# Moving small VectorE and ScalarE work of a four-layer attention kernel to GpSimd, with one load queue and a guarded second program

## The chip, the cores and the metric

The kernel runs on one core of a Trainium2 chip. The metric is device time in microseconds of one launch; the median of a few runs counts. Beside it there is one profiled execution, from which all views of the profile come. Its engines are called PE (TensorE), DVE (VectorE), ACT (ScalarE), POOL (GpSimd) and SP (the engine that issues most DMAs).

## The reference

The input is one sequence of 2048 rows with 512 columns in bfloat16. Four residual layers follow one another: A, B, A, B, where both A layers use the same weights and both B layers use the same weights. There are 32 heads of 16 columns.

```python
def _layernorm(x, axis=-1, eps=1e-5):
    m = jnp.mean(x, axis=axis, keepdims=True); v = jnp.var(x, axis=axis, keepdims=True)
    return (x - m) / jnp.sqrt(v + eps)

def _A_ref(x, wqkv, wo):                       # linear attention
    q, k, v = split(x @ wqkv)                  # (heads, rows, 16)
    phi = lambda t: jnp.where(t > 0, t + 1, jnp.exp(t)) + 1e-6
    pq, pk = phi(q), phi(k)
    kv = einsum("hsd,hse->hde", pk, v);  z = einsum("hsd->hd", pk)
    num = einsum("hqd,hde->hqe", pq, kv)
    den = einsum("hqd,hd->hq", pq, z)[..., None] + 1e-6
    return merge(num / den) @ wo

def _B_ref(x, wqkv, wo):                       # causal window of 256 rows
    q, k, v = split(x @ wqkv)
    scores = einsum("hqd,hkd->hqk", q, k) * (Dh ** -0.5)
    idx = jnp.arange(S)
    mask = (idx[:, None] - idx[None, :] >= 0) & (idx[:, None] - idx[None, :] < 256)
    p = softmax(where(mask, scores, -1e9));  return merge(p @ v) @ wo

x = x + _A_ref(_layernorm(x), A_wqkv, A_wo)
x = x + _B_ref(_layernorm(x), B_wqkv, B_wo)
x = x + _A_ref(_layernorm(x), A_wqkv, A_wo)
x = x + _B_ref(_layernorm(x), B_wqkv, B_wo)
```

## The kernel before

The rows are cut into 16 tiles of 128 rows, which stay in SBUF as `xres` from the first load to the last store. Nothing is a loop on the chip: Python builds a graph of operations, a list scheduler puts every operation on an engine and in an order, and `emit` writes the five instruction streams with semaphore waits. Each engine runs its stream strictly in that order.

The scheduler (`_Sched.schedule`) repeatedly takes, of all operations that could run, the one with the smallest sum of its planned start and `LAM` times its `pick`. `pick` is the operation's place in the graph (about its tile number, counted on through the stages) plus an offset from the table `PLAN`, which has one number for each kind of operation. An operation's engines and assumed times stand beside it, such as `{"DVE": 0.32}`; where two engines are given, the one with the earlier planned start gets it. `LAT` holds the assumed time from the end of an operation on one engine to a start on another. Rings of buffers (`xn`, `E`, `pq`, `kbd`, ...) limit how far one stage may run ahead of the next.

The graph has these stages, which overlap in time:

- "1.": for each tile, layer norm (`ln`), transposition (`transp`), the k and v projections of layer A (`a_kv`), the feature map (`phi`) and the sum of pk and v over all rows (`kv_mm`).
- "2.": for each tile, the q projection of layer A and its output (`a_q`, `a_out`), then layer B's projections (`b_qkv`) and windowed attention (`b_attn`), each ending in `wo`, which transposes, multiplies by the output weight and adds into `xres`. After it "2k." does for the third layer what "1." does for the first.
- "3.": as "2." for the last two layers, with a store of each finished tile.

The lines that matter here:

- `ln`: L587 and L588 take mean and variance on DVE. L589 and L590 form the reciprocal root on ACT as a logarithm and an exponential of one column. L592 normalises into `xn` on DVE. L600 is a DMA transposition issued by SP; L607 is the same on PE for the few tiles listed in `BYPE`.
- `phi`: L647 exponential on ACT into `E`; L648 minimum with one and addition of 1e-6 on DVE, in place; L649 the positive part added on DVE.
- `b_qkv`: L735, two instructions on DVE, multiplies the transposed keys `kT` by two head masks into `kbd`, which is what the scores read. L745 moves `vt` into `vbd` with four DMAs issued by POOL, which wait for the copy at L617.
- `b_attn`: scores on PE (L770, L807), exponentials on ACT (L790, L814), triangular masks as products on DVE (L797 for `pH`, L826 for `pF`), products with v on PE (L838, L850), the reciprocal of the denominators (L860) and the division (L862). The softmax subtracts no maximum.
- `loads`: the 16 row tiles on SP's queue, the weights `w_Ak`, `w_Av`, `w_Aq` on ACT's queue, the other five weights on SP's queue after the rows.
- `consts` and the `fill_` functions: constants and presets, mostly memsets on POOL in the first microseconds.

Of the kernel before, what the change touches and what calls it, by code (L numbers as in the profile page):

```python
# [6 lines left out]
dt = mybir.dt  # L7
# [4 lines left out]
P = 128  # L12
D = 512
# [125 lines left out]
class _Sched:  # L139
# [6 lines left out]
    LAM = 0.033256  # L146
    PAIRS = 4

    def __init__(self, nc, ctx, plan):
        self.nc = nc  # L150
        self.ctx = ctx
        self.plan = plan
        self.ops = []
        self.pools = []
        self.at = ("", 0.0)
        self.handle = {"PE": nc.tensor, "ACT": nc.scalar, "DVE": nc.vector, "POOL": nc.gpsimd, "SP": nc.sync}
# [131 lines left out]
    def emit(self):  # L288
# [39 lines left out]
        sem = {e: self.ctx.enter_context(self.nc.semaphore("s_" + e)) for e in self.ENGS}  # L328
        count = {e: 0 for e in self.ENGS}
        slots = {}  # L330
        for o in order:
            if o.is_dma and getattr(o, "signals", False):
                b = o.refs[-1]
                key = (b.pool.name, b.slot) if b.pool is not None else ("out" if o.final else id(b))
                if key not in slots:
                    slots[key] = [self.ctx.enter_context(self.nc.semaphore("s_dma%d" % len(slots))), 0]
                slots[key][1] += 16 * o.dmas
                o.sem, o.val = slots[key]
# [17 lines left out]
def _dve_cost(n, rate=1):  # L356
# [5 lines left out]
    "1.ln.st": -2.3432, "1.ln.ag": -7.629, "1.ln.ln": 3.7656, "1.ln.rs": -4.4647, "1.ln.xn": -5.7325, "1.ln.xT": -1.1827, "1.ln.xTc": -8.1345, "1.k0":  # L362
    -1.1601, "1.k1": -4.702, "1.k.e": -4.1683, "1.k.m": -6.7525, "1.k.p": -1.6235, "1.v0": 1.4018, "1.v1": 0.4024, "1.vc": -3.4569, "1.kv": -4.203,
    "1.fin0": 2.1358, "1.fin1": -13.6914, "2.q0": 8.2163, "2.q1": 4.674, "2.q.e": 0.348, "2.q.m": 0.4534, "2.q.p": 0.4456, "2.n0": 2.0377, "2.n1":
    -23.4096, "2.da": -0.7298, "2.dr": 2.4131, "2.dm": -1.9393, "2.o.oT": 21.7702, "2.o.w0": 5.1533, "2.o.w1": -9.7692, "2.o.x": 3.8104, "2.b.ln.st":
    4.7152, "2.b.ln.ag": 4.432, "2.b.ln.ln": 1.6702, "2.b.ln.rs": 5.701, "2.b.ln.xn": -1.1144, "2.b.ln.xT": 9.8065, "2.b.k0": 4.5754, "2.b.k1":
    3.6236, "2.b.kc": 2.0847, "2.b.kb": 10.4518, "2.b.q0": 0.8948, "2.b.q1": 2.5577, "2.b.qc": 4.9459, "2.b.v0": 4.9246, "2.b.v1": -12.1234, "2.b.vc":
    5.5499, "2.b.vd": 12.193, "2.a.sH": 0.8556, "2.a.eH0": -2.6845, "2.a.eH1": 0.8974, "2.a.mH0": 0.4401, "2.a.mH1": 3.8097, "2.a.s0": 1.2702,
    "2.a.e00": 1.5581, "2.a.e01": 9.0526, "2.a.m0": -0.62, "2.a.s1": 1.3991, "2.a.e10": 12.4542, "2.a.e11": 7.3125, "2.a.m1": -0.1479, "2.a.s2":
    1.0274, "2.a.e20": 4.7291, "2.a.e21": 4.4722, "2.a.m2": 0.4653, "2.a.s3": 1.7165, "2.a.e30": 1.5475, "2.a.e31": 0.6114, "2.a.m3": -1.3736,  # L370
    "2.a.u0h": 2.7481, "2.a.u00": -34.0427, "2.a.u01": 5.3112, "2.a.dr0": -4.153, "2.a.dm0": -2.6925, "2.a.u1h": 4.975, "2.a.u10": 6.2037, "2.a.u11":
    -18.3104, "2.a.dr1": 6.915, "2.a.dm1": -0.6536, "2.a.o.oT": 14.4848, "2.a.o.w0": 2.4276, "2.a.o.w1": 1.1529, "2.a.o.x": 3.6287, "2.a.o.oTc":
    8.1341, "2k.ln.st": -6.3433, "2k.ln.ag": 0.0878, "2k.ln.ln": 5.2229, "2k.ln.rs": 4.8961, "2k.ln.xn": 3.3782, "2k.ln.xT": 19.3092, "2k.k0": 6.4763,
    "2k.k1": -20.2592, "2k.k.e": -2.6403, "2k.k.m": -3.0627, "2k.k.p": -2.0237, "2k.v0": 6.8601, "2k.v1": 1.882, "2k.vc": 6.6851, "2k.kv": 9.0019,
    "2k.acc": 2.3357, "2k.ln.xTc": -4.0281, "2.fin0": 1.9926, "2.fin1": -9.0356, "3.q0": 17.6187, "3.q1": 11.9424, "3.q.e": -1.6125, "3.q.m": 17.8339,
    "3.q.p": 3.0371, "3.n0": 21.2198, "3.n1": -7.948, "3.da": 12.6926, "3.dr": 3.3151, "3.dm": 6.3971, "3.o.oT": 2.5807, "3.o.oTc": 24.0655, "3.o.w0":
    19.7899, "3.o.w1": 5.4264, "3.o.x": 16.6218, "3.b.ln.st": -10.8173, "3.b.ln.ag": 14.1252, "3.b.ln.ln": 6.9441, "3.b.ln.rs": 21.0639, "3.b.ln.xn":
    12.1622, "3.b.ln.xT": 8.289, "3.b.ln.xTc": 17.8884, "3.b.k0": 15.1594, "3.b.k1": 19.123, "3.b.kc": 14.9965, "3.b.kb": 17.7419, "3.b.q0": 21.072,
    "3.b.q1": 12.1272, "3.b.qc": 18.2848, "3.b.v0": 22.3007, "3.b.v1": 20.3746, "3.b.vc": 17.7903, "3.b.vd": 51.1264, "3.a.sH": 15.3262, "3.a.eH0":
    19.97, "3.a.eH1": 21.9656, "3.a.mH0": 27.1553, "3.a.mH1": 21.5402, "3.a.s0": 14.35, "3.a.e00": 31.3932, "3.a.e01": 18.1646, "3.a.m0": 6.6429,  # L380
    "3.a.s1": 16.293, "3.a.e10": 17.5396, "3.a.e11": 16.9782, "3.a.m1": 24.787, "3.a.s2": 16.1138, "3.a.e20": 20.9056, "3.a.e21": 4.4488, "3.a.m2":
    28.9959, "3.a.s3": 17.2049, "3.a.e30": 0.2397, "3.a.e31": 21.5025, "3.a.m3": 26.0854, "3.a.u0h": 16.3563, "3.a.u00": 5.8543, "3.a.u01": 1.5404,
    "3.a.dr0": 23.5963, "3.a.dm0": 20.2443, "3.a.u1h": 25.5916, "3.a.u10": 15.3421, "3.a.u11": -15.2287, "3.a.dr1": 8.2662, "3.a.dm1": 18.4897,
    "3.a.o.oT": 8.6597, "3.a.o.w0": 26.2182, "3.a.o.w1": 10.8826, "3.a.o.x": 15.5577, "3.a.o.out": -7.4131, "3.a.o.oTc": 16.0395,
}
BYPE = {("x1.", t) for t in range(6)} | {("a2.", 15), ("k2.", 15), ("o3.", 0), ("x3.", 0), ("a3.", 15)}
VMOVE = {"POOL": 2.06}
LATE = 1


class _Kernel:
    def __init__(self, nc, A_x, A_wqkv, A_wo, B_x, B_wqkv, B_wo, out):
# [5 lines left out]
        self.ctx = ExitStack()  # L398
# [13 lines left out]
    def run(self):  # L412
        nc, T = self.nc, self.T
        with self.ctx:
            s = self.s = _Sched(nc, self.ctx, PLAN)
            self.consts()
            self.xres = [_Buf(None, h) for h in self.tiles("xres", T, [P, D])]
            self.stats = self.tiles("stats", 1, [P, T, 6], F32)[0]
            self.mv = self.tiles("mv", 1, [P, T, 2], F32)[0]
            self.rstd = self.tiles("rstd", 1, [P, T], F32)[0]  # L420
            ps = self.ctx.enter_context(nc.psum_tensor("ps", [P, 8, 512], F32))
            self.pG = _Banks("ps", ps)
            s.pools.append(self.pG)
            self.r_xn = self.ring("xn", 4, [P, D])
            self.r_xT = self.ring("xT", 5, [P, 4, P])
            self.r_xTa = self.ring("xTa", T, [P, 4, P])
            self.r_E = self.ring("E", 4, [P, D])
            self.r_pk = self.ring("pk", 8, [P, D])
            self.r_pq = self.ring("pq", 18, [P, 4, P])
            self.r_kvz = self.ring("kvz", 4, [P, 2, 136])  # L430
            self.r_qT = self.ring("qT", 4, [P, 4, P])
            self.r_pF = self.ring("pF", 6, [P, 4, 512])
            self.r_kT = self.ring("kT", 3, [P, 4, P])
            self.r_vt = self.preset("vt", 3, [P, 2, 16, 17], self.fill_vt())
            self.r_o = self.ring("o", 4, [P, D])
            self.r_oT = self.ring("oT", 4, [P, 4, P])
            self.r_dn = self.ring("dn", 4, [P, 32], F32)
            self.kvacc = self.tiles("kvacc", 1, [P, 4, 136], F32)[0]
            self.r_vA = self.preset("vA", 8, [P, 32, 17], self.fill_vA())
            self.r_kbd = self.ring("kbd", 6, [P, 4, 2, P])  # L440
            self.r_vbd = self.preset("vbd", 6, [P, 2, 2, 16, 17], self.fill_vbd())
            self.r_pH = self.preset("pH", 3, [P, 16, 192], self.fill_pH())
            self.loads()
            self.graph()
            s.schedule()
            s.emit()
            done = max((o for o in s.ops if o.final), key=lambda o: o.val)
            nc.sync.wait_ge(done.sem, done.val)
# [36 lines left out]
    def consts(self):  # L485
# [13 lines left out]
        def f_tri(e, en):  # L499
            e.memset(tri[:], 1.0)  # L500
# [31 lines left out]

        s.at = ("", -3)
# [18 lines left out]
    def loads(self):  # L552
# [3 lines left out]
        def dma(key, eng, dst, src, bufs, lat):  # L556
            s.at = ("", key)
            s.op("load", {eng: 0.47}, lambda e, en: e.dma_start(dst, src), writes=bufs, dma=True, tail=lat - s.LAT["SP"][0])

        xv = self.x[0].rearrange("(t p) d -> t p d", p=P)  # L560
        for t in range(T):
            dma(-5 + 0.01 * t, "SP", self.xres[t].h[:], xv[t], [self.xres[t]], 2.4 + 0.2 * t)

        def wload(name, key, eng, c0, c1, lat):
            self._nm = "w_" + name
            h = self.sb([P, 4, c1 - c0])
# [8 lines left out]
        for i, n in enumerate("kqv"):  # L575
            c = "qkv".index(n) * D
            wload("B" + n, -0.9 + 0.01 * i, "SP", c, c + D, 9.0)
# [408 lines left out]
```

## Time and profile before

| | |
|---|---|
| median of 3 runs | 482.95 us (482.86 to 487.02) |
| profiled execution, its own time | 483.88 us |
| span of that execution | 482.6 us |
| mean granted PE clock | 0.968 |
| busy PE, DVE, ACT, POOL | 401.5, 393.7, 384.4, 72.3 us |
| HBM read, written | 6.29 MB, 2.10 MB |

Busy time is the time in which an engine had an instruction under way; the span runs from the first to the last instruction. A group of instructions in the profile gives its line, engine, operation, the tiles written and read with their shapes, the count, the busy time and mean length, and then how long the engine was idle just before such instructions and for whom. The chain of work that ended last is followed back from the last instruction, at each step to whatever released it.

### The profile page before, as it was taken

How to read it: one execution, taken by the hardware profiler on the slowest of the kernel's cores; microseconds unless marked ns; L12 is line 12 of the kernel's file. 1: busy time of each engine (PE TensorE's matmuls, PEld its weight loads, DVE VectorE, ACT ScalarE, POOL GpSimd, SP SyncE). 2: the span in 40 equal slices, each digit the busy share in tenths (PEclk: the TensorE clock that was granted, in tenths of full speed). 3: DMA queues.
4: the chain of work that ended last, by engine and by line, in shares of the span. 5: the costliest groups of instructions: out<-in, count | busy, mean ns of one | idle time of the engine just before them, and what ended most of it. 6: DMA issues, size and time to landing. Idle time of an engine off the chain costs nothing.

```text
span 482.6 us, 18490 instructions
## 1 busy us (share of the span) xinstructions
PE 401.5 (83%) x8173; PEld 279.8 (58%) x8236; DVE 393.7 (82%) x962; ACT 384.4 (80%) x577; POOL 72.3 (15%) x145
## 2 busy tenths in 40 slices
PE   2999898899889898998888887879887878878676
PEld 1546666476666665664655665647665555556444
DVE  6996996989887999885877799789988868877634
ACT  3765367988998889999999446988988878889993
POOL 5000033211211010121100002402211111111100
PEclk9999998999999999997999999999999989999967
DMA  8941252342221223312111012343223343332202
GB/s 270 275 66 23 46 93 56 66 69 47 47 48 37 46 60 66 48 36 48 36 24 25 12 23 55 53 70 55 66 58 58 58 58 58 58 56 48 48 25 45
DMA packets 76656, 29.39 MB, mean 61 GB/s; under 512 B 66336, under 2 KB 74528, under 8 KB 76576
## 3 DMA queue, kind: packets, MB, share of 16 engines
q1 hardware_dynamic: 70896, 22.17, 23.3%
q0 software_dynamic: 4096, 4.46, 5.8%
q10 hardware_dynamic: 1584, 1.57, 1.0%
q8 instruction: 65, 1.06, 1.0%
q14 instruction: 15, 0.12, 0.1%
HBM read 6.29 MB, written 2.10 MB: 17 GB/s over the span
## 4 chain that ended last, share of the span: by engine, by line
DVE 30%; PE 29%; ACT 22%; DMA 16%; issue 2%; SPq 0%
ACT pF L814 15%; PE ps L626 13%; DMA oT<-o 9%; PE ps L638 6%; ACT pH L790 4%; DVE stats L587 4%; DVE xres L657 4%; PE ps L850 4%; DMA xT<-xn 3%; DVE o L717 3%; DVE pF L826 3%; DMA xTa<-xn 3%; PE ps L838 2%; PE ps L807 2%; DVE pq L649 2%
## 5 line engine op out<-in xcount | busy, mean ns | idle before, releaser
L814 ACT ACTIVATE pF<-ps 128x1024 bf16<-128x1024 f32 (+2 forms) x256 | 241.6, 971 | 21.0 <-PE ps L807 18.6
L745 POOL DMA_DIRECT2D vbd<-vt x128 | 66.2, 526 | 377.7 <-DVE vt L617 184.1
L790 ACT ACTIVATE pH<-ps 128x1024 bf16<-128x1024 f32 (+1 forms) x64 | 62.2, 972 | 10.7 <-PE ps L770 9.4
L807 PE MATMUL ps<-qT,kbd 32*128 32x128 bf16 x1920 | 51.9, 223 | 21.2 <-ACT pF L814 12.2
L657 DVE TENSOR_TENSOR xres<-ps,xres 128x512 bf16<-128x512 f32 x64 | 43.6, 683 | 22.8 <-PE ps L626 22.7
L647 ACT ACTIVATE E<-ps 128x512 bf16<-128x512 f32 x64 | 38.2, 597 | 29.7 <-PE ps L638 15.8
L807 PEld LDWEIGHTS ps<-qT,kbd 32*128 32x128 bf16 x1920 | 30.3, 95 | 53.4 <-ACT pF L814 31.4
L850 PE MATMUL ps<-vbd,pF 128*128 128x34 bf16 x1920 | 59.4, 179 | 0.0
L826 DVE TENSOR_TENSOR pF<-pF,const 128x512 bf16<-128x512 bf16 (+1 forms) x128 | 50.8, 398 | 7.3 <-ACT pF L814 6.7
L850 PEld LDWEIGHTS ps<-vbd,pF 128*128 128x128 bf16 x1920 | 53.8, 97 | 0.4
L626 PE MATMUL ps<-w_Bo,oT 128*128 128x512 bf16 x120 | 34.5, 408 | 16.1 <-DMA oT<-o 10.8
L797 DVE TENSOR_TENSOR pH<-pH,const 128x1024 bf16<-128x1024 bf16 (+1 forms) x64 | 41.8, 653 | 7.4 <-ACT pH L790 6.4
L587 DVE BATCH_NORM_STATS2 stats<-xres 128x6 f32<-128x512 bf16 x64 | 43.8, 687 | 3.7 <-DMA xres<-in_A_x_dram 2.5
L838 PE MATMUL ps<-vbd,pH 128*128 128x34 bf16 x960 | 34.9, 179 | 4.7 <-DVE pF L826 2.7
L626 PE MATMUL ps<-w_Ak,xTa 128*128 128x512 bf16 x117 | 32.4, 401 | 6.7 <-DMA xTa<-xn 4.4
L638 PE MATMUL ps<-xT,w_Bk 128*128 128x128 bf16 x512 | 35.9, 221 | 2.0 <-DMA xT<-xn 0.8
L638 PE MATMUL ps<-xT,w_Bq 128*128 128x128 bf16 x512 | 35.5, 223 | 1.8 <-DMA xT<-xn 1.3
L838 PEld LDWEIGHTS ps<-vbd,pH 128*128 128x128 bf16 x960 | 29.6, 97 | 11.8 <-DVE pF L826 4.2
L626 PE MATMUL ps<-w_Ao,oT 128*128 128x512 bf16 x111 | 29.1, 379 | 7.1 <-DMA oT<-o 3.6
L638 PE MATMUL ps<-xTa,w_Aq 128*128 128x128 bf16 x512 | 34.1, 219 | 0.1
L638 PEld LDWEIGHTS ps<-xT,w_Bk 128*128 128x128 bf16 x512 | 30.0, 99 | 6.9 <-issue 1.7
L626 PE MATMUL ps<-w_Av,xTa 128*128 128x512 bf16 x123 | 33.2, 388 | 0.5 <-issue 0.2
(70 smaller groups left out, 544.9 us busy)
## 6 DMA issues: line engine op xcount, KB each, us to landing
vbd<-vt POOLq DMA_DIRECT2D x128, 34.0 KB, 2.4
xres<-in_A_x_dram SPq DMA_DIRECT2D x16, 128.0 KB, 6.4
out_dram<-xres SPq DMA_DIRECT2D x16, 128.0 KB, 1.7
oT<-o SPq DMA_TRANSPOSE x61, 2.5
w_Ak<-in_A_wqkv_dram ACTq DMA_DIRECT2D x1, 512.0 KB, 4.8
w_Av<-in_A_wqkv_dram ACTq DMA_DIRECT2D x1, 512.0 KB, 6.6
w_Aq<-in_A_wqkv_dram ACTq DMA_DIRECT2D x1, 512.0 KB, 8.9
w_Ao<-in_A_wo_dram SPq DMA_DIRECT2D x1, 512.0 KB, 7.0
```

The lines of the kernel that those rows point to most:

```text
L587: s.op(n + ".st", {"DVE": 0.595}, lambda e, en: e.bn_stats(a_st, x.h[:]), reads=[x], writes=[st])
L626: i = e.matmul(g.h, xT.h[:, kt, :], w.h[:, kt, :], start=(kt == 0), stop=(kt == 3), skip_group_check=True)
L638: i = e.matmul(g.h[:, f * P:(f + 1) * P], w.h[:, kt, f * P:(f + 1) * P], xT.h[:, kt, :], start=(f == 0 and kt == 0), stop=(kt == 3), skip_ ...
L657: s.op(n + ".x", {"DVE": _dve_cost(512)}, lambda e, en: e.tensor_tensor(x.h[:], g.h, x.h[:], ALU.add), reads=[g], writes=[x])
L745: return [e.dma_start(vbd.h[64 * a:64 * a + 64, j, a], vt.h[64 * j:64 * j + 64, a]) for a in range(2) for j in range(2)]
L790: return e.activation(d, c, ACT.Exp, bias=0.0, scale=DH ** -0.5)
L797: return e.tensor_tensor(vH(g), vH(g), tr, ALU.mult)
L807: i = e.matmul(ss[r // 2].h[:, r % 2, m * P:m * P + P], kbds[fj[m] // 2].h[32 * r:32 * r + 32, f, fj[m] % 2, :], qT.h[32 * r:32 * r + 32, ...
L814: s.op("e%d%d" % (f, g), {"ACT": _act_cost(2 * (4 - m0) * P)}, lambda e, en, S=ss[g], pb=pb, g=g: e.activation(pb.h[:, 2 * g:2 * g + 2, m0 ...
L826: return e.tensor_tensor(v, v, tr, ALU.mult)
L838: i = e.matmul(U.h[:, c:c + 34], pH.h[:, 4 * r + f, 64 * a:64 * a + P], vbds[j // 2].h[:, j % 2, :, 4 * f + r, :], start=first[0], stop=Tr ...
L850: i = e.matmul(U.h[:, c:c + 34], pFs[f].h[:, r, m * P:m * P + P], vbds[fj[m] // 2].h[:, fj[m] % 2, :, 4 * f + r, :], start=False, stop=Tru ...
```

## The change

Six things change. The reciprocal root is formed on POOL by an addition and a power of minus one half. The key masks go to POOL; `xn` and the first step of the feature map may go to POOL or DVE. All loads go out on SP's queue in one written order. The triangular masks become a minimum with 0 or 3e38. The reciprocals of the softmax denominators are kept for all tiles; their extremes are compared with two limits, a count is formed, and every engine reads it at its end: if it is above zero, a second program with bounded scores runs behind the first. For the given inputs only the first program's work and the branch are executed. Last, the scheduler gets a new `LAM`, a new `PLAN` (every offset differs), a margin of 0.5 us on the assumed time of transpositions and of the `vbd` move, and slightly smaller rings, and SBUF is laid out anew.

```diff
-    LAM = 0.033256
+    LAM = 0.036392
...
 VMOVE = {"POOL": 2.06}
+XN = {"POOL": 0.62, "DVE": 0.32}
+EM = {"POOL": 0.62, "DVE": 0.2}
+KB = {"POOL": 1.2}
 LATE = 1
+SLACK = 0.5
...
+            with ExitStack() as self.ctx:
+                s = self.build()
+                done = max((o for o in s.ops if o.final), key=lambda o: o.val)
+                for e in s.handle.values():
+                    e.wait_ge(self.verdict.sem, self.verdict.val)
+                v = nc.values_load(self.flag[0:1, 0:1], min_val=0, max_val=1 << 20)
+                nc.sync.wait_ge(done.sem, done.val)
+            with nc.If(v > 0):
+                nc.all_engine_barrier()
+                self.safe = True
+                with ExitStack() as self.ctx:
+                    s = self.build()
...
-            self.r_pq = self.ring("pq", 18, [P, 4, P])
+        self.r_pq = self.ring("pq", 17, [P, 4, P])
...
-            self.r_dn = self.ring("dn", 4, [P, 32], F32)
+        self.r_dn = self.ring("dn", 3, [P, 32], F32)
...
-            e.memset(tri[:], 1.0)
+            e.memset(tri[:], BIG)
...
+            dma("SP", h[:], src[:, :, c0:c0 + D], [b], 1.2 if name[1] != "k" and name != "Av" else 0.5, 1.55)
...
+        for k in (0, 1, "Ak", 2, 3, "Av", *range(4, T), "Aq", "Ao", "Bk", "Bq", "Bv", "Bo"):
+            wload(k) if isinstance(k, str) else xload(k)
...
-        s.op(n + ".ln", {"ACT": 0.12}, lambda e, en: e.activation(a_rs, self.mv[:, t, 1:2], ACT.Ln, bias=LN_EPS), reads=[mv], writes=[rs])
-        s.op(n + ".rs", {"ACT": 0.12}, lambda e, en: e.activation(a_rs, a_rs, ACT.Exp, bias=0.0, scale=-0.5), writes=[rs])
+        s.op(n + ".ln", {"POOL": 0.2}, lambda e, en: e.tensor_scalar(a_rs, self.mv[:, t, 1:2], LN_EPS, None, op0=ALU.add), reads=[mv], writes=[rs])
+        s.op(n + ".rs", {"POOL": 0.2}, lambda e, en: e.tensor_tensor(a_rs, a_rs, self.half.h[:], ALU.pow), reads=[self.half], writes=[rs])
...
-        s.op(n + ".xn", {"DVE": 0.32}, ...
+        s.op(n + ".xn", XN, ...
...
-            s.op(n, {"SP": 1.25}, ..., dma=True)
+            s.op(n, {"SP": 1.25}, ..., dma=True, tail=SLACK)
...
-        s.op(n + ".m", {"DVE": 0.2}, ...
+        s.op(n + ".m", EM, ...
...
-        s.op("kb", {"DVE": 0.525}, kb, reads=[kT, self.mab], writes=[kbd])
+        s.op("kb", KB, kb, reads=[kT, self.mab], writes=[kbd])
...
-        s.op("vd", VMOVE, vd, reads=[vt], writes=[vbd], dma=True, tail=0.4).dmas = 4
+        s.op("vd", VMOVE, vd, reads=[vt], writes=[vbd], dma=True, tail=0.4 + SLACK).dmas = 4
...
-                return e.tensor_tensor(vH(g), vH(g), tr, ALU.mult)
+                return e.tensor_tensor(vH(g), vH(g), tr, ALU.min)
...
-                return e.tensor_tensor(v, v, tr, ALU.mult)
+                return e.tensor_tensor(v, v, tr, ALU.min)
...
-            dn = self.r_dn.buf()
+            dn = _Buf(None, self.rden[:, int(last), t, 16 * g:16 * g + 16])
+            self.dens[int(last)].append(dn)
...
-        s.op("table", {"ACT": 1.3}, lambda e, en: e.preload_act_table_set("natural_log_exp_and_others"))
+        s.op("table", {"ACT": 1.3}, lambda e, en: e.preload_act_table_set("exp_and_others"))
...
+    def judge(self, b2):
+        ...
+        for i, (lay, lo, hi, at) in enumerate(((0, 0, T, b2 + 3), (1, 0, 7, b2 + 9), (1, 7, 12, b2 + 14), (1, 12, T - 1, b2 + T + 2), (1, T - 1, T, b2 + T + 6))):
+            ...
+            for k, fn in enumerate((ALU.max, ALU.min)):
+                s.op("ext%d%d" % (i, k), {"DVE": _dve_cost(32 * (hi - lo))}, lambda e, en, v=v, i=i, k=k, fn=fn: e.tensor_reduce(
+                    self.ext[:, k, i:i + 1], v, axis=mybir.AxisListType.X, op=fn), reads=src, part=[ext])
+        s.op("far0", {"DVE": 0.1}, ...
+        s.op("far1", {"DVE": 0.1}, ...
+        s.op("count", {"PE": 0.06}, ...
+        self.verdict = s.op("flag", {"DVE": 0.1}, ...
```

## The prediction

> **What bounds the kernel now.** I read the engine sums first, then busy time by stage, then the groups of instructions by shape, then the chain of work inside the stages that are least full, then the first microseconds of the timeline.
>
> ```profile
> PE 401.5 (83%) x8173; PEld 279.8 (58%) x8236; DVE 393.7 (82%) x962; ACT 384.4 (80%) x577; POOL 72.3 (15%) x145
> ```
>
> Three engines are within 4% of each other and GpSimd (POOL) is idle. An average says little, so the same by stage (width, then busy time of PE, PEld, DVE, ACT, POOL, then clock, DMA share, GB/s):
>
> ```profile
> 9.00:45.00 36.00, 34.57 (x215) 18.25 (x220) 30.34 (x81) 23.53 (x61) 0.00 (x0) 1.00 0.59 151
> 85.00:220.00 135.00, 120.79 (x2658) 84.62 (x2675) 120.98 (x295) 121.57 (x178) 22.61 (x45) 1.00 0.29 51
> 345.00:429.00 84.00, 67.66 (x1666) 47.80 (x1679) 69.84 (x163) 70.90 (x85) 14.33 (x28) 0.98 0.36 58
> 429.00:459.00 30.00, 22.63 (x673) 16.90 (x673) 19.78 (x45) 27.93 (x32) 4.10 (x8) 0.96 0.18 43
> ```
>
> While only PE is heavily loaded (9 to 45) it is busy 96% of the time. Where PE, DVE and ACT carry the same load (85 to 220) all three stop at 90%; from 345 to 429, 81 to 84%. The difference is waiting on each other. From 429 on, ACT's exponentials set the pace (93%). The groups the change touches:
>
> ```profile
> L826 DVE TENSOR_TENSOR pF<-pF,const 128x512 bf16<-128x512 bf16 x112 | 46.2, 414 | 5.6 <-ACT pF L814 5.1
> L797 DVE TENSOR_TENSOR pH<-pH,const 128x1024 bf16<-128x1024 bf16 x56 | 38.5, 688 | 7.3 <-ACT pH L790 6.4
> L592 DVE TENSOR_SCALAR xn<-xres,mv,rstd 128x512 bf16<-128x512 bf16 x64 | 25.0, 396 | 0.1
> L735 DVE TENSOR_SCALAR kbd<-kT,const 128x512 bf16<-128x512 bf16 x64 | 19.6, 348 | 0.7 <-ACT kT L617 0.2
> L648 DVE TENSOR_SCALAR E<-E 128x512 bf16<-128x512 bf16 x64 | 18.2, 286 | 11.7 <-ACT E L647 11.5
> L590 ACT ACTIVATE rstd<-rstd 128x1 f32<-128x1 f32 x64 | 12.7, 200 | 0.9
> L589 ACT ACTIVATE rstd<-mv 128x1 f32<-128x1 f32 x64 | 12.6, 199 | 9.6 <-DVE mv L588 9.1
> ```
>
> One turn of the chain between 345 and 429, which repeats about every 12 us (start, length, what):
>
> ```profile
> 358.39 0.70 DVE kT L617
> ...
> 359.12 0.62 DVE kbd L735 x2
> ...
> 362.04 0.24 DVE xn L592
> ...
> 363.14 4.71 DMA oT<-o
> ```
>
> The key masks and the normalising stand in this chain: 0.86 us of each turn. Last, what GpSimd does to VectorE when both work, and the only elementwise work GpSimd has here:
>
> ```profile
> 1.29 0.29 POOL L496 TENSOR_SCALAR_AFFINE_SELECT const<-const 128x128 bf16<-128x128 bf16 x1 [0.28 <-issue]
> 3.43 0.23 POOL L505 TENSOR_SCALAR_AFFINE_SELECT const<-const 64x64 bf16<-64x64 bf16 x1
> 5.70 1.67 POOL L483 MEMSET pH<- 128x1536 f32 x1
> 6.89 0.62 DVE L592 TENSOR_SCALAR xn<-xres,mv,rstd 128x512 bf16<-128x512 bf16 x1
> 8.71 0.40 DVE L592 TENSOR_SCALAR xn<-xres,mv,rstd 128x512 bf16<-128x512 bf16 x1
> ```
>
> The xn that began inside GpSimd's memset took 0.62 us and ended just after it (7.51 against 7.37); a free one takes 0.40. The two engines get in each other's way.
>
> **The change, part by part.**
>
> *Taken from ACT:* 64 logarithms and 64 exponentials of one column, 12.6 + 12.7 = 25.3 us (384 to 359). Besides their own time they queue: in the turn above the logarithm runs at 358.33 and its exponential at 361.35, behind three 1.02 us exponentials, so xn starts at 361.96 though its mean was there at 357.8.
>
> *Taken from DVE*, by the spacing to the next start rather than the busy time: xn 64 x 0.32 = 20.5, E 64 x 0.20 = 12.8, two kbd halves 32 x 0.53 = 17.0; at most 50.3 us (394 to 343). The key masks have only GpSimd to go to; xn and E may go to either, whichever the planner sees start first. GpSimd, nearly empty, should usually win; if half go back the relief is 34.
>
> *Put on GpSimd:* 192 instructions of 128x512 (64 xn, 64 E, 64 mask halves) and 128 of one column. No such row exists. From below: the two selections above differ by 64 elements and about 0.05 us, 0.8 ns an element, so 512 cost about 0.6 us. From above: the memset of vA, 256 strided elements in 1.18 us, 4.6 ns an element, gives 2.4. The first is the same kind of work (dense bf16 read and written), so I take 0.6. One column: 0.1 (the one-column memsets) to 0.5, taken as 0.2; the power itself is not in the trace. Sum: 72 + 192 x 0.6 + 128 x 0.2 = 213 us, 44% of the span; at 2.4 it would be over 550 and GpSimd the bound.
> The Trainium skill, GPSIMD Engine Reference (Elementwise, side-by-side cycle accounting), gives 0.77 us for 512 elements in a tight loop; by that figure GpSimd's load would be an estimated 246 us, still below the others.
>
> *Collisions.* The masks on DVE (128 at L826, 64 at L797) read two tensors from SBUF. If a GpSimd instruction of length d makes such a mask wait out its rest, it holds 192d/483 = 0.40d of the time, and the 192 masks wait d/2 each when hit: 38 d² us of DVE. At 0.6 that is 14 us, which leaves DVE near 357.
>
> *What is queued behind.* GpSimd's sequencer waits today for vt ahead of each vbd group (184.1 + 177.6 us behind DVE's and ACT's copies), and nobody suffers, since only vbd is behind. Now roots, xn and masks are behind, and xT, the projections and the scores wait for them. The planner places these by expected times, so only lateness of vt against the plan is paid. Bounds: nothing, to a whole group's issue, 2.05 us, for each of 32 groups; I take 0.1 each, 3 us, within the slack of the stages below.
>
> *Loads.* Today 16 row loads on SP and three weights on ACT run together, and the second and third rows land only at 6 to 8 us; PE's first projection is at 9.56. In one ordered queue rows 0 and 1 lead, then w_Ak. Worth 0 to 4 us, taken as 2: the roots then wait among GpSimd's memsets (busy to 7.4 today), which keeps part. SP's own queue: its loads are issued by 14.4 us today, three weights more at 0.5 to 1.3 us each make it 16 to 18, and its first transpose stands at 19.1; past that, each microsecond would delay xTa. The later weights are first used beyond 40 us.
>
> *Masks by minimum instead of product:* same shapes. A minimum already runs in L648 at 0.29 us for 512 elements, so I take no price; from above, at the pace of DVE's casts (0.69 us for 512) the 192 masks would cost 69 us more, an end beyond C below. Reciprocals kept in a fixed tile cost nothing: the same instruction writes elsewhere.
>
> *The check:* ten reductions over the reciprocals, 2 x (512 + 224 + 160 + 96 + 32) elements at about 1 ns plus start, some 3 us of DVE spread over the run. Only the last two, two comparisons, one tiny matmul and one reduction follow the last reciprocal (476.44), about 1.5 us; the final transpose, projection and store run until 482.6 and cover them. Without that cover they cost those 1.5. Not covered: SP's branch past the second program after the last store. Bounds 0 to 3 (a fetched instruction packet on the instruction queue occupies a DMA engine for about 77/65 = 1.2 us, plus about 1.7 to land, as the stores do); taken 1.5.
>
> *By stage.* Start: -2. 9 to 45: PE is at 96%, -0.5. 45 to 85: DVE and PE tie, -2.5. 85 to 220: PE 120.8 is the floor; with the others about 10% lighter its fill rises half way from 90% to the 96% of stage one, 120.8/0.93 = 130, -5. 220 to 260, ACT-bound at 93%: -2. 260 to 300, DVE first: -3. 300 to 345: -2.5. 345 to 429: seven turns x 0.86 us, -6. From 429: one root pair, -0.5. Sum -24. Against it: +1.5 for the end, and of 14 us of collisions DVE's 30% share of the chain, +4. Span 482.6 - 24 + 5.5 = 464.1; with the 1.3 us that the profiled execution has outside the span, 465.4; the median of the runs is 0.2% below that execution, so **464.5 us**.
>
> **Rivals.**
> *A, PE becomes the only bound.* If everything fills as in stage one outside the ramps, 401.5/0.96 = 418 plus some 20 us of start and ACT-bound tail: 440. For it: GpSimd's idleness, and roots that no longer queue behind exponentials. Against: DMA transposes of 3 to 5 us remain in the chain, 37.6% of it from 345 to 429.
> *B, the relief buys little.* All work keeps the wait pattern of the new order, PE stays at 83 to 84%, vt holds up GpSimd's queue for 0.3 us a group more (10 us), or half of xn and E return to DVE: 24 falls to about 5, and with the end 1.5 and collisions 4 the time is 483. For it: transposes and PE untouched; against: kbd and xn stand in the chain itself.
> *C, slower: the shared path of GpSimd and VectorE.* One mechanism, 38 d². It equals the 50 us of relief at d = 1.15 us; at 1.3 it is 65, DVE ends 14 us above today's load, and the time is near 497. For it: the 0.62 us xn. Against: 0.6 from the nearest row is half of the deciding point.
> The Trainium skill, SBUF — State Buffer (Who interferes with whom), has this as an exclusive lock between a GpSimd instruction that reads SBUF and a VectorE one with two SBUF inputs; the xn row agrees that one waits out the other, but that instruction has one SBUF tensor, and no run here shows a mask beside GpSimd reading.
>
> **How the numbers follow.** Forecast 0.54, A 0.14, B 0.12, C 0.20. The forecast alone spans 452 to 476 (the loads' and end's bounds, collisions from 0 to all 14, half the stage gains). No more than 2 in 10 left out, and 0.6 to 1.3 us for the unmeasured GpSimd price, widen it to 444 to 496. About 1% is what a measurement of this kernel can tell. Faster by over 1% (below 478): forecast, A and a trace of B, 0.69; within 1%: 0.10; slower: C and the rest of B, 0.21.
>
> **What would show it.** Right: POOL about 210 us with 128x512 instructions near 0.6 us; ACT near 359, DVE 345 to 360; PE 85 to 88% of the span; one turn of the late chain near 11 us without kbd and xn; first projection near 7.5 us; the last stores still last, with 1 to 2 us behind them. Wrong: GpSimd instructions above 1.1 us, masks at L826 and L797 clearly longer than 0.41 and 0.69, or long waits of xn for roots queued behind vbd (then C or B); PE above 91% (then A).

## The result and the profile after

The changed kernel takes 557.4 us (median of 4 runs, 553.9 to 559.8) against 482.9 us. The ratio is 1.151, with an interval of 1.143 to 1.160. The forecast was 464.5 us in a range of 444 to 496, faster; the kernel became 74 us slower. Where some runs of a kernel were in a slower state with a lower clock, its ratio is formed without them. Each ratio is against the kernel before as it ran beside that kernel (medians of 480.4 to 484.1 us). Its profiled execution has a span of 555.7 us at a mean PE clock of 0.909.

The engine sums of the profile after:

```profile
PE 426.1 (77%) x8175; PEld 296.9 (53%) x8237; DVE 378.2 (68%) x825; ACT 373.7 (67%) x449; POOL 403.9 (73%) x425
```

ACT and DVE are lighter, as intended. GpSimd (POOL) went from 72 to 404 us, not to the forecast 213. PE does the same work; its busy time rose about as much as its mean clock fell (401.5 x 0.968 / 0.909 = 428). The groups by shape (busy time, mean ns of one, then the idle time before):

```profile
L636 POOL TENSOR_SCALAR xn<-xres,mv,rstd 128x512 bf16<-128x512 bf16 x58 | 123.3, 2126 | 5.4 <-POOL rstd L634 0.7
L779 POOL TENSOR_SCALAR kbd<-kT,const 128x512 bf16<-128x512 bf16 x64 | 102.6, 1612 | 43.1 <-DVE kT L661 41.6 <-ACT kT L661 1.0
L692 POOL TENSOR_SCALAR E<-E 128x512 bf16<-128x512 bf16 x28 | 54.0, 1930 | 16.8 <-ACT E L691 14.7
L634 POOL TENSOR_TENSOR rstd<-rstd,const 128x1 f32<-128x1 f32 x64 | 36.7, 578 | 3.4
L633 POOL TENSOR_SCALAR rstd<-mv 128x1 f32<-128x1 f32 x64 | 14.7, 236 | 48.4 <-DVE mv L632 42.3 <-DVE dn L758 5.0
L888 DVE TENSOR_TENSOR pF<-pF,const 128x512 bf16<-128x512 bf16 x112 | 49.4, 441 | 22.3 <-ACT pF L876 21.3
L858 DVE TENSOR_TENSOR pH<-pH,const 128x1024 bf16<-128x1024 bf16 x56 | 42.1, 752 | 8.0 <-ACT pH L851 7.3
```

A 128x512 instruction takes 1.6 to 2.1 us on GpSimd, where 0.6 was assumed. The planner had put 58 xn, 28 E and all key masks there: 150 instructions, 280 us. The triangular masks on VectorE, which rival C expected to suffer, grew only from 414 to 441 and from 688 to 752 ns. The chain that ended last, by engine and by line:

```profile
POOL 41%; PE 21%; ACT 16%; DVE 10%; DMA 7%; issue 4%; POOLq 0%
POOL xn L636 15%; ACT pF L876 13%; POOL E L692 9%; PE ps L670 8%; POOL kbd L779 7%; PE ps L682 5%; POOL rstd L634 5%; DMA xT<-xn 4%; POOL vbd L789 3%; DMA xTa<-xn 3%; PE ps L912 3%; ACT pH L851 2%; PE ps L868 2%; POOL rstd L633 2%; DVE xres L701 2%
```

Before, GpSimd had no entry there. A stretch of that chain in order of time shows the queue:

```profile
76.61 1.05 POOL rstd L634 x2
77.66 2.08 POOL xn L636
79.82 1.95 POOL E L692
...
82.16 0.58 POOL rstd L634
...
82.84 2.08 POOL xn L636
...
87.02 1.92 POOL E L692
```

Each xn waits for the E instructions of the tiles ahead and the other way round; PE is down to 9.7 busy microseconds in the 20 from 80 to 100. Elsewhere the others wait for GpSimd or for what it holds up (waiter, who ended the wait, total, times, longest):

```profile
DVE pq L693 <- POOL E L692: 24.8, 19, 4.2
PEld ps L868 <- POOL kbd L779: 16.4, 8, 5.5
PEld ps L682 <- DMA xT<-xn: 15.3, 11, 3.4
```

### The profile page after: what moved, and what is told of

It reads as the page before. It is cut to its first block, busy times and chain, and to the rows that moved or that the text cites. A ratio compares the mean times of both kernels' runs of the same rounds, so it can differ in the third digit from the quotient of the medians.

```text
span 555.7 us, 18521 instructions
## 1 busy us (share of the span) xinstructions
PE 426.1 (77%) x8175; PEld 296.9 (53%) x8237; DVE 378.2 (68%) x825; ACT 373.7 (67%) x449; POOL 403.9 (73%) x425
## 4 chain that ended last, share of the span: by engine, by line
POOL 41%; PE 21%; ACT 16%; DVE 10%; DMA 7%; issue 4%; POOLq 0%
POOL xn L636 15%; ACT pF L876 13%; POOL E L692 9%; PE ps L670 8%; POOL kbd L779 7%; PE ps L682 5%; POOL rstd L634 5%; DMA xT<-xn 4%; POOL vbd L789 3%; DMA xTa<-xn 3%; PE ps L912 3%; ACT pH L851 2%; PE ps L868 2%; POOL rstd L633 2%; DVE xres L701 2%
## 5 line engine op out<-in xcount | busy, mean ns | idle before, releaser
L779 POOL TENSOR_SCALAR kbd<-kT,const 128x512 bf16<-128x512 bf16 x64 | 102.6, 1612 | 43.1 <-DVE kT L661 41.6
L636 POOL TENSOR_SCALAR xn<-xres,mv,rstd 128x512 bf16<-128x512 bf16 x58 | 123.3, 2126 | 5.4 <-POOL rstd L634 0.7
L888 DVE TENSOR_TENSOR pF<-pF,const 128x512 bf16<-128x512 bf16 (+1 forms) x128 | 54.2, 423 | 33.7 <-ACT pF L876 32.7
L692 POOL TENSOR_SCALAR E<-E 128x512 bf16<-128x512 bf16 x28 | 54.0, 1930 | 16.8 <-ACT E L691 14.7
L858 DVE TENSOR_TENSOR pH<-pH,const 128x1024 bf16<-128x1024 bf16 (+1 forms) x64 | 46.2, 722 | 15.6 <-ACT pH L851 14.7
L633 POOL TENSOR_SCALAR rstd<-mv 128x1 f32<-128x1 f32 x64 | 14.7, 236 | 48.4 <-DVE mv L632 42.3
L682 PE MATMUL ps<-xT,w_Bq 128*128 128x128 bf16 x512 | 41.4, 240 | 10.0 <-DMA xT<-xn 9.5
L670 PE MATMUL ps<-w_Ak,xTa 128*128 128x512 bf16 x115 | 35.6, 438 | 13.6 <-DMA xTa<-xn 10.5
L682 PE MATMUL ps<-xT,w_Bk 128*128 128x128 bf16 x512 | 42.1, 243 | 4.2 <-DMA xT<-xn 4.2
L682 PEld LDWEIGHTS ps<-xT,w_Bq 128*128 128x128 bf16 x512 | 35.1, 109 | 14.2 <-DMA xT<-xn 10.5
L682 PEld LDWEIGHTS ps<-xT,w_Bk 128*128 128x128 bf16 x512 | 35.7, 110 | 10.0 <-DMA xT<-xn 4.8
```

The costliest lines, as they stand in the source:

```text
L636: s.op(n + ".xn", XN, lambda e, en: e.tensor_scalar(xn.h[:], x.h[:], self.mv[:, t, 0:1], a_rs, op0=ALU.subtract, op1=ALU.mult), reads=[x, ...
L670: i = e.matmul(g.h, xT.h[:, kt, :], w.h[:, kt, :], start=(kt == 0), stop=(kt == 3), skip_group_check=True)
L682: i = e.matmul(g.h[:, f * P:(f + 1) * P], w.h[:, kt, f * P:(f + 1) * P], xT.h[:, kt, :], start=(f == 0 and kt == 0), stop=(kt == 3), skip_ ...
L692: s.op(n + ".m", EM, lambda e, en: e.tensor_scalar(E.h[:], E.h[:], 1.0, 1e-6, op0=ALU.min, op1=ALU.add), writes=[E])
L779: i = e.tensor_scalar(kbd.h[:, :, :, a * 64:a * 64 + 64], src, self.mab.h[:, a:a + 1], None, op0=ALU.mult)
L888: return e.tensor_tensor(v, v, tr, ALU.min)
```

## The experiments

**The same order, shorter GpSimd instructions.** The theory is that only the length of GpSimd's large instructions is at fault. The rival is that the new order, the loads or the check are, with GpSimd merely standing beside them. A constant written into the same tile has about the assumed length (lines shortened at the dots).

```diff
-        s.op(n + ".xn", XN, lambda e, en: e.tensor_scalar(xn.h[:], ...
+        s.op(n + ".xn", XN, lambda e, en: e.memset(xn.h[:], 0.5) if en == "POOL" else e.tensor_scalar(xn.h[:], ...
...
-        s.op(n + ".m", EM, lambda e, en: e.tensor_scalar(E.h[:], ...
+        s.op(n + ".m", EM, lambda e, en: e.memset(E.h[:], 0.5) if en == "POOL" else e.tensor_scalar(E.h[:], ...
...
-                i = e.tensor_scalar(kbd.h[:, :, :, a * 64:a * 64 + 64], src, self.mab.h[:, a:a + 1], None, op0=ALU.mult)
+                i = e.memset(kbd.h[:, :, :, a * 64:a * 64 + 64], 0.01)
```

> The changed kernel with every instruction of all five engines in the same order and with the same waits; only GpSimd's xn, E and kbd instructions write a constant into the whole tile instead of computing it (their arithmetic is left out). A bf16 constant of 512 columns should take about 0.6 us, the length that the prediction assumed. Theory 1 (the length of GpSimd's instructions, 1.6 to 2.1 us, is the cause): 455 to 480 us, as forecast. Rival (the new order, the load queue or the check is the cause, and GpSimd only stands next to it): 530 to 555 us.

It took 468.6 us, ratio 0.972 (0.966 to 0.977). Engine sums and chain of this kernel, and its instructions (least, median and greatest ns):

```profile
PE 398.4 (85%) x8175; PEld 280.9 (60%) x8237; DVE 365.4 (78%) x825; ACT 370.1 (79%) x449; POOL 199.9 (43%) x425
ACT 42%; PE 33%; DVE 13%; POOL 4%; issue 4%; DMA 3%; POOLq 0%; SPq 0%
```

```profile
L636 POOL MEMSET xn<- x58: 514/524/597, 6.2 to 434.1; 128x512 bf16 x58
L692 POOL MEMSET E<- x28: 514/524/585, 11.3 to 288.0; 128x512 bf16 x28
L779 POOL MEMSET kbd<- x64: 518/524/670, 69.1 to 443.2; 128x512 bf16 x64
```

At 0.52 us each the order of the changed kernel is within 4 us of the forecast, and GpSimd within 13 us of its forecast load. So the 89 us between 557 and 469 come from what GpSimd does in those 150 instructions, and no other part has to be blamed. Whether it is their length or their reading is the next question.

**The same length, no reading.** Rival C blamed the shared path: GpSimd reading SBUF while a mask reads two tensors. Writing the constants repeatedly holds GpSimd nearly as long without a read (`E` is changed as `xn` is).

```diff
+def _rep(e, ap, val, n):
+    for k in range(n):
+        if k:
+            e.drain()
+        i = e.memset(ap, val)
+    return i
...
-        s.op(n + ".xn", XN, lambda e, en: e.tensor_scalar(xn.h[:], ...
+        s.op(n + ".xn", XN, lambda e, en: _rep(e, xn.h[:], 0.5, 3) if en == "POOL" else e.tensor_scalar(xn.h[:], ...
...
-                i = e.tensor_scalar(kbd.h[:, :, :, a * 64:a * 64 + 64], src, self.mab.h[:, a:a + 1], None, op0=ALU.mult)
+                i = _rep(e, kbd.h[:, :, :, a * 64:a * 64 + 64], 0.01, 3 - a)
```

> As the kernel with constants instead of xn, E and kbd on GpSimd, in the same order, but each constant is written three times with a drain between (kbd halves three times and twice), so that GpSimd is held about 2.0 us for xn and E and 3.3 us for a kbd pair without reading SBUF; the arithmetic is left out. Theory 1 (how long GpSimd is held decides): 540 to 570 us. Rival C of the prediction (what hurts is GpSimd reading SBUF while VectorE reads two tensors): below 500 us.

It took 546.9 us, ratio 1.133 (1.126 to 1.141). GpSimd's span of xn was 1.78 us (two in 3.56), of a kbd pair about 2.9, so it was held some 30 us less than in the changed kernel, and the kernel ended 10.5 us earlier. The masks in this run, and the chain by engine (POOLq is GpSimd's own sequencer at the drains):

```profile
L896 DVE TENSOR_TENSOR pF<-pF,const 128x512 bf16<-128x512 bf16 x112 | 47.0, 420 | 25.1 <-ACT pF L884 24.0
L866 DVE TENSOR_TENSOR pH<-pH,const 128x1024 bf16<-128x1024 bf16 x56 | 38.4, 686 | 8.0 <-ACT pH L859 7.3
POOL 24%; POOLq 18%; issue 17%; ACT 15%; PE 12%; DVE 8%; DMA 5%
```

Without GpSimd reading, the masks are back at 420 and 686 ns. The masks' collisions with GpSimd's reading were thus 2.4 + 3.7 = 6 us of VectorE in the changed kernel, and taking them away hardly helped. The constants have small collisions of their own: VectorE's 36 E took 391 ns on average, against 362 in the changed kernel and 286 in the kernel before, its 6 xn 569 against 860 and 396. That is some 5 us in either kernel. The time GpSimd is held decides.

**The same order, VectorE in GpSimd's place.** After planning, the large instructions are issued by VectorE at the same places; nothing is planned anew. (`safe` marks the second program, which does not run here.)

```diff
         s.schedule()
+        if not safe:
+            for o in s.ops:
+                if o.name.endswith(("ln.xn", "q.m", "k.m", "b.kb")):
+                    o.eng = "DVE"
         s.emit()
```

> The changed kernel with its planned order kept in every engine; only the xn, E and kbd instructions that stood on GpSimd are issued by VectorE at the same planned places. So the offsets, the loads, the check and the roots on GpSimd are as in the changed kernel, and nothing is planned anew. Theory 1 (the length of GpSimd's large instructions is the cause): 470 to 495 us. Rival (this order is bad whatever engine does the work): 515 us or more.

It took 477.2 us, ratio 0.986 (0.983 to 0.989): 80 us less than the changed kernel and 1.4% less than the kernel before, a small gain, yet its interval ends below 1, with the load queue, the check, the minimum masks, the new order and the roots on GpSimd all in place.

```profile
PE 401.6 (84%) x8175; PEld 282.4 (59%) x8237; DVE 399.3 (84%) x975; ACT 371.0 (78%) x449; POOL 126.1 (26%) x275
ACT 36%; PE 30%; DVE 27%; issue 3%; DMA 3%; SPq 0%; POOL 0%
```

GpSimd, now with roots and `vbd` only, has left the chain.

**One kind at a time.** As in that version, but only xn, or only the key masks, stay on GpSimd (the tuple of names above is shortened by one).

> The changed kernel's planned order; of the large instructions only xn stays on GpSimd (58 of 2.1 us), E and kbd are issued by VectorE at the same places. Theory 1: xn has 15 of the 31 hundredths of the chain that the three kinds had, so about half of the 80 us between 477 and 557: 505 to 525 us.

> The changed kernel's planned order; of the large instructions only kbd stays on GpSimd (64 of 1.6 us), xn and E are issued by VectorE at the same places. Theory 1: kbd had 7 of 31 hundredths: 485 to 505 us.

With xn alone 508.8 us, ratio 1.052 (1.044 to 1.060); with the key masks alone 499.6 us, ratio 1.039 (1.030 to 1.048). Against the 0.986 without either, that is 6.6 and 5.3 hundredths, 32 and 26 us. The full loss is 1.151 - 0.986 = 16.5 hundredths, 80 us, so about 22 us are left for E and for the three meeting in one queue; E alone was not run. The chains by engine:

```profile
POOL 24%; ACT 24%; PE 20%; DVE 18%; DMA 11%; issue 3%; POOLq 0%; SPq 0%
```

```profile
PE 31%; ACT 25%; DVE 24%; POOL 14%; DMA 3%; issue 2%; SPq 0%
```

The first is with xn, the second with the key masks. The masks' share is smaller than their price suggests; which waits make up the rest was not followed.

**The roots.** In the version at 477 us the roots go back to ScalarE, at the same planned places (`o.eng = "ACT"`, logarithm and exponential).

> The changed kernel's planned order; xn, E and kbd on VectorE as in the version at 477 us, and the roots on ScalarE as logarithm and exponential at the same planned places. If roots on GpSimd are a gain by ScalarE's relief of 25 us: 482 to 495 us. If they are a loss through 0.8 us of latency: below 475 us.

480.0 us, ratio 0.994 (0.990 to 0.998) against 0.986: the roots on GpSimd are worth 3 to 4 us in this order, with intervals that barely part. The result lies between the two expected bands; the sign is that of the first, the size is below it. In the order of the kernel before, the same move does not pay (the two operations become the addition and the power of the changed kernel):

```diff
             s.schedule()
+            for o in s.ops:
+                if o.name.endswith("ln.ln") or o.name.endswith("ln.rs"):
+                    o.eng = "POOL"
...
```

> The kernel before with its order kept; only the two one-column instructions of each reciprocal root are issued by GpSimd, at the same planned places, 0.24 and 0.58 us each. ScalarE loses 25 us of work. If ScalarE's relief counts and GpSimd has time to spare: 470 to 482 us. If the longer root (0.8 us instead of 0.4) with its two hops sits on the chain: 484 us or more.

The ratio is 1.016 (1.009 to 1.022), from two runs of 488.7 and 493.8 us: the second band, though with only two runs the size is loose. The key masks alone, moved the same way in the order of before:

> The kernel before with its order kept; only the key masks are issued by GpSimd, at the same planned places, 1.56 us for each half, instead of VectorE's 0.53 for both. VectorE loses 17 us, each kbd comes about 2.6 us later, 32 times. If that delay is covered by other work: 478 to 486 us. If the scores wait for it, as the waits on kbd in the profile after suggest: 490 to 530 us.

491.6 us, ratio 1.017 (1.015 to 1.020), at the lower end of the second band. PE waited for kbd before the scores only twice, 3.6 us in all, and GpSimd holds 2% of the chain, so that the scores wait is shown for a part of the 8 us alone. The same move costs 26 us in the changed kernel's order: what a late kbd costs depends on the order too, and that order was planned with 1.2 us for a pair that takes 3.2.

**Planned anew.** Four kernels changed an engine or a price ahead of the planner, which then made another order. In the first, all of GpSimd's new work goes back (`XN = {"DVE": 0.32}`, `EM = {"DVE": 0.2}`, `KB = {"DVE": 0.525}`, roots on ScalarE):

> The changed kernel with xn, E and kbd on VectorE and the roots on ScalarE as before; the load queue, the check, the masks by minimum and the new planner offsets stay. Theory 1 (length of GpSimd's instructions): 478 to 495 us, about the time before. Rival (offsets, loads or check are the cause): 530 us or more.

> The changed kernel with xn, E and kbd on VectorE; only the roots stay on GpSimd (0.24 and 0.58 us each, 52 us in all). Theory 1: 470 to 490 us, GpSimd about 130 us busy; if the roots alone were a main part of the loss, well above 500 us.

> The changed kernel with the planner told what the profile after shows: 2.1 us for xn, 1.93 for E, 3.2 for the two kbd halves, 0.23 and 0.57 for the root on GpSimd; kbd may go to VectorE too. Theory 1 in the form that the wrong assumed price misled the order: 470 to 490 us, with few of the large instructions left on GpSimd. Rival (GpSimd's work on the chain is harmful wherever it stands, even well placed): above 500 us.

> The kernel before plus the one load queue, the check with its second program, the masks by minimum and the smaller rings; roots on ScalarE, xn, E and kbd on VectorE, with the old planner offsets, old weight and no margin. If these parts cost nothing, as the prediction priced them (2 us gained at the start, 1.5 lost at the end): 478 to 486 us. If the check or the loads are part of the loss: 490 us or more.

They took 527.1 (ratio 1.094, 1.089 to 1.099), 514.3 (1.069, 1.062 to 1.075), 529.6 (1.099, 1.093 to 1.105) and 514.6 us (1.063, 1.060 to 1.066), far from every number that the first theory gave. The third was no test of its question: told the true prices, the planner still left GpSimd 334 us busy, because it takes the engine with the earliest start; GpSimd has 6% of the chain there, so that run is not held back by GpSimd's queue as the changed kernel is. For the first two the plan is the cause: their work is that of the versions at 480 and 477 us, on the same engines but for some copies (6 and 12 more on ScalarE), and what else differs is the order. The fourth has the old offsets with the new loads, check, masks and rings; these parts cost nothing in the order kept at 480 us, so it is likely the order again, but no run keeps its order and takes a part out. Why those orders are worse, and by which waits, was not followed up; it stays open.

## Why the prediction was wrong

**The step that failed** is the price in "Put on GpSimd": "The first is the same kind of work (dense bf16 read and written), so I take 0.6". Two selections of 128 and 64 columns were stretched to 512 by a slope of 0.8 ns an element. Measured were 2.13 us for xn, 1.93 for E and 1.61 for a kbd half, inside the bounds of 0.6 to 2.4 but near the end that was set aside. The selections pick elements and do not compute on them; the spread between the three goes with what the instruction does: one operation for kbd, two with fixed numbers for E, two with a scalar per row for xn. The power took 0.58 us, beyond the 0.5 of its upper bound. Together GpSimd's load was 404 us instead of 213. The text had said what the upper end would do ("at 2.4 it would be over 550 and GpSimd the bound") and then closed its range at 496: the bounds of an unknown cost were not carried into the range.

**The rest of the sum came out about right**, as the run with 0.52 us instructions shows: 468.6 against 464.5. Part of that is luck: of the 18 us to be gained it has 12 to 14, with both reliefs smaller than priced and no masks held up, since constants read nothing. The terms, one by one:

- *ACT's relief* was 11.5 us, not 25.3: 382.5 busy with the roots on ScalarE against 371.0 without, in the same order. The 128 one-column instructions lie partly over their neighbours, so their lengths added up are more than the time they take.
- *DVE's relief* in that run was 399.3 - 365.4 = 34 us, not 50. The planner left 36 of 64 E and 6 of 64 xn on VectorE, a third of them; the text had named 34 for a half.
- *Collisions* were 6 us of masks, not 14, and some 5 us of VectorE's own xn and E, for which the text had no term. Rival C had the sign and the critical length right (d above 1.15 us means slower) and, of the mechanism, the half that a mask waits for GpSimd; but the mask waits only for the first 0.6 us of the instruction, not for the rest of its length (rows in the last section). By 38 d² the masks would have lost 133 us at d = 1.87. In its place GpSimd's own queue took the largest part of the chain (41%), which the text knew only as an aside. The rule cited for it, the exclusive lock in the Trainium skill, SBUF — State Buffer (Who interferes with whom), agrees with the trace for that first part: a mask beside a GpSimd xn took up to 0.83 us instead of 0.41. In the rest of GpSimd's 2.08 us the masks ran freely.
- *What is queued behind* vt: GpSimd's idle time before vbd fell from 378 to 17 us; no loss shows there. What did stand behind one another were xn, E and kbd.
- *Loads*: no gain. The first statistics ran at 2.97 instead of 3.23, but the first projection at 9.82 instead of 9.56, behind a 2.08 us xn on GpSimd. With a 0.52 us constant there it began at 8.14, 1.4 us earlier than before, where 2 were forecast.
- *The check*: as priced. The last addition ends 3.0 us before the end (552.7 of 555.7), against 1.7 before (480.9 of 482.6), 1.2 us more for a forecast 1.5; its instructions are covered.

Rivals A and B fell with the price: PE went to 77%, not above 91%, and the relief was not small but paid for many times over.

## What to carry to other kernels

A moved instruction has to be priced on the engine it moves to by a row of its own kind and size; where no such row exists, the upper bound belongs in the range, and one run of that instruction is worth more than all the rest of the sum. An idle engine is not free capacity when it stands in the chain of every tile: instructions of 0.3 to 0.4 us on a full VectorE cost 80 us of kernel time as 1.6 to 2.1 us on an empty GpSimd. To test a part of a planned kernel, keep the planned order and swap the engine under it; two kernels planned anew for other prices, with the old ones' offsets, were 37 and 47 us slower than kept orders with nearly the same work on each engine.

## What the runs showed of the hardware

GpSimd's instructions took longer with more operations in them: at 128x512 bf16 a constant took 0.52 us, one operation 1.56, two with fixed numbers 1.93, two with scalars per row 2.08 (medians); one column took 0.23 and a power of one column 0.57.

GpSimd and VectorE keep each other waiting for a part of an instruction. Rows of the timeline after:

```profile
178.47 2.08 POOL L636 TENSOR_SCALAR xn<-xres,mv,rstd 128x512 bf16<-128x512 bf16 x1
178.67 0.83 DVE L888 TENSOR_TENSOR pF<-pF,const 128x512 bf16<-128x512 bf16 x1 [0.72 <-ACT pF L876]
454.73 0.69 DVE L858 TENSOR_TENSOR pH<-pH,const 128x1024 bf16<-128x1024 bf16 x1
454.92 2.46 POOL L636 TENSOR_SCALAR xn<-xres,mv,rstd 128x512 bf16<-128x512 bf16 x1
456.53 0.41 DVE L888 TENSOR_TENSOR pF<-pF,const 128x512 bf16<-128x512 bf16 x1
```

A mask at L888 that began early in a GpSimd xn ended at one point: the five that began 0.20 to 0.50 us after it took 0.83 to 0.53 us and all ended 1.03 us after its start, so each waited until 0.62 us of the 2.08 were over. The sixteen that began 0.61 to 1.63 us after it took their usual 0.41 to 0.43. Beside GpSimd's half of a kbd, the wait lasts to 0.55 us. The other way round, a GpSimd xn that began while a mask ran took 2.46 us instead of 2.08 (third and fourth row).

VectorE's xn and E, which read one tensor, wait too. Its six xn beside a GpSimd xn began 0.02 to 0.12 us after it, took 0.80 to 0.88 us instead of 0.40, and all ended 0.90 to 0.91 us after its start. At the end of GpSimd's instruction they wait once more, as masks do not: three E that began 1.50, 1.72 and 1.93 us after the start of a GpSimd xn took 0.74, 0.52 and 0.30 us, and each ended 0.15 us after it. A constant they wait out: in the run with repeated constants, 20 xn and E of VectorE met one and ended 0.14 to 0.15 us after it, while masks there kept their lengths. And beside the run of GpSimd memsets at the start, a VectorE instruction that took 0.17 us in other runs lasted 3.10, until the last memset ended:

```profile
8.12 3.10 DVE L569 TENSOR_SCALAR const<-const 128x8 f32<-128x8 int32 x1
8.34 1.17 POOL L509 MEMSET vA<- 128x256 bf16 x1
9.12 0.80 POOL L512 MEMSET vt<- 128x96 bf16 x1
9.52 1.67 POOL L521 MEMSET pH<- 128x1536 f32 x1
12.63 2.07 POOL L636 TENSOR_SCALAR xn<-xres,mv,rstd 128x512 bf16<-128x512 bf16 x1
12.65 0.88 DVE L636 TENSOR_SCALAR xn<-xres,mv,rstd 128x512 bf16<-128x512 bf16 x1 [0.42 <-POOL rstd L634]
```

The last memset ends at 11.19 and the instruction at 11.22; the last two rows are one of the six pairs of xn.
